# Decoding 64-bit weight words on ScalarE and VectorE: six engine steps rewritten as three

## The chip, the core and the metric

The kernel runs on one core of a Trainium2 chip. The metric is the time of one execution on the device in microseconds (us). A run's time is given as a median of several runs; the profile is one execution of its own, recorded by the hardware profiler.

## The reference

Pooled attention feeds two feed-forward stages. The attention inputs are float32, the five weight matrices are float64.

```python
q_pool = q.reshape(B, H, S // 2, 2, D).mean(axis=3)          # B, H, S, D = 4, 8, 1152, 64
attn = softmax(scale * q_pool @ k.T)                         # 576 queries, 1152 keys per head
x = (attn @ v)  ->  rows of 512, 2304 of them
h = x @ w_in;  x1 = max(0.01 * h, h) @ w_out                 # 512 -> 2048 -> 512
h = max(x1 @ w1, x1 @ w2, x1 @ w3);  out = h @ moe2_w_out    # 512 -> 768 -> 512
```

## The kernel before

Attention works through 16 pairs of heads, four pairs to each of the four batches. For a tile of 128 queries TensorE (PE) makes the scores `s`, VectorE (DVE) takes the row maximum `mx` (line 335), ScalarE (ACT) the exponential `p` (line 336). PE transposes `p` into `pst` and `psf`; ACT copies the first (line 378) and DVE the second (line 385) into `pt`, which PE multiplies with the values (`pv`). Preparing the next pair's keys and queries (`psk`, `psq`, `kt`, `q`) needs PE, ACT (lines 221, 256) and DVE (lines 224, 260). From the fifth pair on there is one score buffer, so the next scores wait for the exponential of the last.

The two feed-forward stages of a batch (`experts`) are interleaved with the attention of the next batch: a generator hands out their matmuls (`m`, `o`) at a fixed ratio to the attention's. The weights are cut into 56 chunks of 128 x 512 numbers. Every activation and every weight is kept as two float32r halves, a rounded one and the rest, and a product is three matmuls.

During batch 0 each chunk is decoded once. `decoded` (line 576) loads it as pairs of 32-bit words into `wraw` (three buffers; line 581, on the SP queue, 512 KB) and turns the pairs into float32 in `wmant` (two buffers). `split_chunk` (line 609) makes the two halves `wsplit` out of it, by a cast on ACT (line 617) and a subtraction on GpSimd (POOL, line 618), and stores them to a scratch buffer in device memory (line 626). Batches 1 to 3 load the halves back. `chunk` keeps the decode 3.75 chunks ahead of its use.

The six steps of `decoded` before, for the words `high` and `low` of a float64:

- line 591, DVE: the 20 fraction bits of `high`, with a one ahead of them, as an integer `m`
- line 594, DVE: `low * 2**-32 + m`, the fraction as a float32, written over `low`
- line 597, DVE: the 11 exponent bits of `high`, into `m`
- line 600, ACT: the exponent shifted to its place in a float32 and re-biased (bias tile `ebias`)
- line 601, DVE: the sign of `high` joined to it, written over `high`
- line 604, POOL: fraction times power of two, into `m`

So `wraw` comes free when line 604 has ended, and `wmant` is held from line 591 to the end of line 618.

Each engine runs its queue in order. The order in the queues is made when the program is built: a scheduler plays the program through with durations of its own and places each instruction where it expects its inputs; the code's order breaks ties, and maxima and exponentials are moved ahead by `tc.high_priority`. A queue so laid out doesn't reorder on the chip: an instruction whose input is late holds all that stand behind it.

Of the kernel before, what the change touches and what calls it, by code (L numbers as in the profile page):

```python
# [7 lines left out]
F32 = mybir.dt.float32  # L8
F32R = mybir.dt.float32r
I32 = mybir.dt.int32  # L10
U32 = mybir.dt.uint32
I64 = mybir.dt.int64
ACTF = mybir.ActivationFunctionType
ALU = mybir.AluOpType
# [8 lines left out]
def kernel(  # L23
# [21 lines left out]
    nc = tc.nc  # L45
# [19 lines left out]
    scale = 0.5 / float(D) ** 0.5  # L65
    NOSYNC = mybir.DependencyInfo(mybir.DependencyClass.NoSync, mybir.DependencyReason.DATA)

    const = ctx.enter_context(tc.tile_pool(name="const", bufs=1))
# [23 lines left out]
    s_mid = ps_5.tile([128, 512], F32, name="s1")  # L92

    ident = const.tile([128, 128], F32, name="ident")
    ebias = const.tile([128, 1], F32, name="ebias")
    rb = [const.tile([128, w], F32, name=f"rb{w}") for w in (X0, T - X0)]
    qt = {}
    for j in range(2):
# [49 lines left out]
    def gap(j):  # L148
        return X0 - 64 * j
# [426 lines left out]
    def decoded(src):  # L576

        raw = wr_p.tile([128, 512, 2], I32, tag="wr", bufs=3, name="wraw")  # L580
        load = nc.sync.dma_start(out=raw.rearrange("p (a f) w -> p a (f w)", a=src.shape[1]), in_=src)
        if len(early) < 2:
            early.append(tc.add_manual_dep(
                load.ins, marks[GATE],
                mybir.DependencyInfo(mybir.DependencyClass.Sync, mybir.DependencyReason.DATA),
                reason="weights behind the first pair",
            ))
        low, high = raw[:, :, 0], raw[:, :, 1]
        m = wr_p.tile([128, 512], I32, tag="wm", name="wmant")
        mf = m.bitcast(F32)  # L590
        nc.vector.tensor_scalar(  # L591
            out=m, in0=high, scalar1=0xFFFFF, scalar2=0x100000, op0=ALU.bitwise_and, op1=ALU.bitwise_or
        )
        nc.vector.scalar_tensor_tensor(  # L594
            out=low.bitcast(F32), in0=low.bitcast(U32), scalar=2.0 ** -32, in1=m, op0=ALU.mult, op1=ALU.add
        )
        nc.vector.tensor_scalar(  # L597
            out=m, in0=high, scalar1=20, scalar2=0x7FF, op0=ALU.logical_shift_right, op1=ALU.bitwise_and
        )
        nc.scalar.activation(out=m, in_=m, func=ACTF.Relu, scale=float(1 << 23), bias=ebias)  # L600
        nc.vector.scalar_tensor_tensor(  # L601
            out=high, in0=high, scalar=-0x80000000, in1=m, op0=ALU.bitwise_and, op1=ALU.bitwise_or
        )
        nc.gpsimd.tensor_tensor(out=mf, in0=low.bitcast(F32), in1=high.bitcast(F32), op=ALU.mult)  # L604
        return mf

    stores = []

    def split_chunk(c):
        src = chunks[c]  # L610
        if wide:
            r = decoded(src)
        else:
            r = wr_p.tile([128, 512], F32, tag="wm", name="wmant")
            nc.sync.dma_start(out=r.rearrange("p (a f) -> p a f", a=src.shape[1]), in_=src)
        t = w_p.tile([128, 2, 512], F32R, tag="w", name="wsplit")
        nc.scalar.copy(out=t[:, 0], in_=r)  # L617
        nc.gpsimd.tensor_tensor(out=t[:, 1], in0=r, in1=t[:, 0], op=ALU.subtract)  # L618
        stores.append((c, t))
        wt[c] = t  # L620
        if len(stores) > 1:
            store_chunk()
# [173 lines left out]
    if True:  # L796
        nc.gpsimd.memset(ident, 0.0)
        nc.gpsimd.affine_select(
            out=ident, in_=ident, pattern=[[-1, 128]], compare_op=ALU.not_equal, fill=1.0, base=0, channel_multiplier=1
        )  # L800
        nc.gpsimd.memset(ebias, -float((1023 - 127 + 20) << 23))
        nc.gpsimd.memset(rb[0][:, 256:X0], 1.0)
        for j in range(2):
            for part in range(2):
                nc.gpsimd.memset(qt[j, part][:, gap(j):gap(j) + 64].bitcast(F32), 0.0)
        moe = None
        roomy = True
        batch = 0
        spent = [0.0, 0.0]

        def advance():
            nonlocal roomy, moe
            d = next(moe, None)
            if d is None:
                moe = None
            elif d == "room":
                roomy = True
            else:
                spent[1] += d

        for c in attention():
            if c == "room":
                while not roomy:
                    advance()
                continue
            if c == "batch":
                while moe is not None:
                    advance()
                moe = experts(batch)
                roomy = False  # L830
                batch += 1
                spent[:] = [0.0, 0.0]
                continue
            done, want = c
            spent[0] += done
            goal = spent[0] * RATIO
            if want is not None:
                goal = min(goal + AHEAD, spent[1] + want)
            while moe is not None and spent[1] < goal:
                advance()  # L840
        while moe is not None:
            advance()
# [30 lines left out]
```

## Time and profile before

| | us |
|---|---|
| median of 3 runs | 1373.49 (1372.48 to 1377.55) |
| span of the profiled execution | 1378.4 |
| PE busy, share of the span | 1274.7 (92%) |
| DVE busy | 729.2 (53%) |
| ACT busy | 638.0 (46%) |
| POOL busy | 357.9 (26%) |

The chunks are decoded between 54 and 539 us, 54 of the 56 after 180 us. The slices of the span in which DVE is busiest (up to 9 tenths) lie in that part; in the second half of the span DVE falls to 4 or 5 tenths and later to 1 or 2. The PE row is lowest in the first third. A share of the whole span is therefore an average over parts with different limits, and the stretch from 180 to 540 us is the one to read. The profiled execution is 4.9 us longer than the median of the timed runs.

### The profile page before, as it was taken

Reading aid. Unit: us, or ns where it says so; the run is one execution under the profiler, and the core shown is the slowest. Engines: PE = TensorE matmul, PEld = TensorE weight load, DVE = VectorE, ACT = ScalarE, POOL = GpSimd, SP = SyncE. Lnnn points to the kernel's source line nnn. Section 1 sums busy time; section 2 is a strip of 40 time slices with the busy share of each in tenths; the row PEclk is TensorE's granted clock in tenths of the full one; section 3 lists DMA queues with packets and bytes.
Section 4 is the critical chain, followed back from the end, with each engine's and each line's share of the span. In section 5 each row is a group of like instructions: output and inputs, shape, how many; then the busy total and the mean of one; then the engine's idle time right before and its main releaser. Section 6 shows DMA issues by size and latency. Waiting matters only on the chain.

```text
span 1378.4 us, 19366 instructions
## 1 busy us (share of the span) xinstructions
PE 1274.7 (92%) x7376; PEld 1024.7 (74%) x7376; DVE 729.2 (53%) x1218; ACT 638.0 (46%) x1253; POOL 357.9 (26%) x322
## 2 busy tenths in 40 slices
PE   5888878789889899999999989999999999999998
PEld 4556646577667678777778868777777788888888
DVE  5756466788897796454645453545555401222110
ACT  5667665556556555353545444444454432112111
POOL 1111034565574554111122110121120102224110
PEclk9999989899899999999999999999999999999999
DMA  5423053756656565353535353443433345333343
GB/s 155 121 73 74 0 148 106 209 199 188 204 190 191 198 205 185 120 155 125 162 124 157 118 149 119 143 142 124 151 121 117 109 138 171 122 123 125 108 134 108
DMA packets 86904, 193.31 MB, mean 140 GB/s; under 512 B 11292, under 2 KB 41756, under 8 KB 86812
## 3 DMA queue, kind: packets, MB, share of 16 engines
q1 hardware_dynamic: 86812, 192.08, 44.6%
q8 instruction: 58, 0.95, 0.3%
q14 instruction: 34, 0.28, 0.1%
HBM read 146.80 MB, written 35.13 MB: 132 GB/s over the span
## 4 chain that ended last, share of the span: by engine, by line
PE 72%; DVE 13%; issue 5%; ACT 5%; POOL 3%; DMA 1%; POOLq 0%; ACTq 0%; DVEq 0%; SPq 0%
PE m L109 38%; PE pv L109 11%; PE s L109 10%; PE pst L109 6%; PE o L109 6%; DVE mx L335 2%; DVE wraw L594 2%; DMA qraw<-in_q_dram 1%; DVE wmant L591 1%; POOL wsplit L618 1%; DVE mx L325 1%; DVE wmant L597 1%; DVE q L260 1%; DVE pt L385 1%; POOL wmant L604 1%
## 5 line engine op out<-in xcount | busy, mean ns | idle before, releaser
L109 PE MATMUL m<-x,w 128*128 128x512 f32 x1224 | 309.6, 398 | 0.0
L109 PEld LDWEIGHTS m<-x,w 128*128 128x128 f32 x1224 | 223.3, 189 | 54.5 <-issue 13.1
L378 ACT COPY pt<-pst 128x512 f32<-128x512 f32 x288 | 167.3, 586 | 187.2 <-PE pst L109 186.2
L109 PE MATMUL s<-kt,q 128*128 128x384 f32 x840 | 190.8, 360 | 27.1 <-ACT p L336 15.0
L335 DVE TENSOR_REDUCE mx<-s 128x1 f32<-128x1152 f32 x108 | 146.3, 1354 | 114.9 <-PE s L109 114.6
L109 PE MATMUL pst<-ident,p 128*128 128x128 f32 x1080 | 170.8, 279 | 14.5 <-DVE pt L385 7.4
L109 PEld LDWEIGHTS s<-kt,q 128*128 128x128 f32 x840 | 149.6, 196 | 38.5 <-ACT p L336 17.0
L109 PEld LDWEIGHTS pst<-ident,p 128*128 128x128 f32 x1080 | 132.7, 143 | 52.6 <-issue 11.9
L739 POOL TENSOR_TENSOR g<-t,g 128x512 fp32r<-128x512 f32 x64 | 84.1, 1315 | 336.5 <-DVE g L738 336.5
L336 ACT ACTIVATE p<-s,mx 128x1152 f32<-128x1152 f32 x108 | 132.3, 1225 | 82.6 <-DVE mx L335 81.8
L109 PE MATMUL pv<-pt,v 128*64 128x320 f32 (+1 forms) x1008 | 154.0, 445 | 12.7 <-DVE pt L385 12.4
L109 PE MATMUL m<-g,w 128*128 128x512 f32 x576 | 149.8, 399 | 0.0
L109 PEld LDWEIGHTS m<-g,w 128*128 128x128 f32 x576 | 103.7, 188 | 24.5 <-issue 6.2
L109 PEld LDWEIGHTS pv<-pt,v 128*64 128x64 f32 x1008 | 69.3, 146 | 70.5 <-issue 22.8
L109 PE MATMUL m<-x,wsplit 128*128 128x512 f32 x408 | 107.4, 403 | 1.2 <-ACT t L765 0.7
L737 ACT ACTIVATE t<-m 128x512 f32<-128x512 f32 x80 | 44.4, 555 | 123.7 <-PE m L109 123.5
L109 PEld LDWEIGHTS m<-x,wsplit 128*128 128x128 f32 x408 | 74.0, 189 | 21.3 <-issue 4.4
L738 DVE CAST g<-t 128x512 fp32r<-128x512 f32 x64 | 32.8, 512 | 102.7 <-ACT t L737 102.2
L618 POOL TENSOR_TENSOR wsplit<-wmant,wsplit 128x512 fp32r<-128x512 f32 x56 | 77.0, 1380 | 34.3 <-ACT wsplit L617 32.2
L604 POOL TENSOR_TENSOR wmant<-wraw 128x512 f32<-128x512 f32 x56 | 61.6, 1100 | 93.3 <-DVE wraw L601 82.1
L677 POOL TENSOR_TENSOR y<-t,y 128x512 fp32r<-128x512 f32 x24 | 32.1, 1339 | 202.1 <-ACT y L676 202.0
L767 DVE TENSOR_TENSOR t<-m,t 128x512 f32<-128x512 f32 (+1 forms) x60 | 38.2, 636 | 84.2 <-PE m L109 73.3
(110 smaller groups left out, 1657.0 us busy)
## 6 DMA issues: line engine op xcount, KB each, us to landing
w<-w SPq DMA_DIRECT2D x168, 512.0 KB
w<-wsplit SPq DMA_DIRECT2D x56, 512.0 KB
wraw<-in_moe_w_out_dram SPq DMA_DIRECT2D x22, 512.0 KB
wraw<-in_moe_w_dram SPq DMA_DIRECT2D x18, 512.0 KB
qraw<-in_q_dram SPq DMA_DIRECT2D x15, 576.0 KB
kraw<-in_k_dram SPq DMA_DIRECT2D x15, 576.0 KB
q<-q SPq DMA_DIRECT2D x52, 160.0 KB
wraw<-in_moe_w_in_dram SPq DMA_DIRECT2D x16, 512.0 KB
```

Source lines behind the costliest of these rows:

```text
L109: mm = f(*args, **kwargs)
L335: nc.vector.tensor_reduce(out=mx[:, 0:1], in_=ps[:, :, 0:SN], axis=AX.XY, op=ALU.max, negate=True)
L336: nc.scalar.activation(out=p[2], in_=ps[:, :, 0:SN], func=ACTF.Exp, bias=mx[:, 0:1], accum_out=rs[:, i:i + 1])
L378: nc.scalar.copy(out=dst, in_=ps.rearrange("p (j c) -> p j c", j=2))
L594: nc.vector.scalar_tensor_tensor(out=low.bitcast(F32), in0=low.bitcast(U32), scalar=2.0 ** -32, in1=m, op0=ALU.mult, op1=ALU.add)
L604: nc.gpsimd.tensor_tensor(out=mf, in0=low.bitcast(F32), in1=high.bitcast(F32), op=ALU.mult)
L618: nc.gpsimd.tensor_tensor(out=t[:, 1], in0=r, in1=t[:, 0], op=ALU.subtract)
L677: nc.gpsimd.tensor_tensor(out=t[:, 1], in0=src, in1=t[:, 0], op=ALU.subtract)
L737: nc.scalar.activation(out=t, in_=ps[:, 0:k.n], func=ACTF.Prelu, alpha=0.01)
L738: nc.vector.tensor_copy(out=gt[:, 0], in_=t)
L739: nc.gpsimd.tensor_tensor(out=gt[:, 1], in0=t, in1=gt[:, 0], op=ALU.subtract)
L767: nc.vector.tensor_tensor(out=t, in0=ps[:, 0:k.n], in1=t, op=ALU.max)
```

## The change

The decode becomes three steps. ACT reads `high` as a float32 and applies a parametric ReLU in place: positive numbers are multiplied by 2^-112, negative ones by 2^-80, which re-biases the exponent field and turns the sign into an exponent bit that the shift below moves to the sign's place. DVE reduces `low` in place to its three top bits, as an integer of 0 to 7. DVE then shifts `high` left by three, joins the three bits, and writes `m`, whose bits are the float32. The tile `ebias` goes, and with it its memset at the start; the line numbers of the changed kernel are one lower ahead of `decoded` and seven lower behind it.

```diff
-        mf = m.bitcast(F32)
-        nc.vector.tensor_scalar(
-            out=m, in0=high, scalar1=0xFFFFF, scalar2=0x100000, op0=ALU.bitwise_and, op1=ALU.bitwise_or
-        )
-        nc.vector.scalar_tensor_tensor(
-            out=low.bitcast(F32), in0=low.bitcast(U32), scalar=2.0 ** -32, in1=m, op0=ALU.mult, op1=ALU.add
-        )
-        nc.vector.tensor_scalar(
-            out=m, in0=high, scalar1=20, scalar2=0x7FF, op0=ALU.logical_shift_right, op1=ALU.bitwise_and
-        )
-        nc.scalar.activation(out=m, in_=m, func=ACTF.Relu, scale=float(1 << 23), bias=ebias)
-        nc.vector.scalar_tensor_tensor(
-            out=high, in0=high, scalar=-0x80000000, in1=m, op0=ALU.bitwise_and, op1=ALU.bitwise_or
-        )
-        nc.gpsimd.tensor_tensor(out=mf, in0=low.bitcast(F32), in1=high.bitcast(F32), op=ALU.mult)
-        return mf
+        nc.scalar.activation(
+            out=high.bitcast(F32), in_=high.bitcast(F32), func=ACTF.Prelu, scale=2.0 ** -112, alpha=2.0 ** 32
+        )
+        nc.vector.tensor_scalar(
+            out=low, in0=low.bitcast(U32), scalar1=2.0 ** -29, scalar2=7.0, op0=ALU.mult, op1=ALU.min
+        )
+        nc.vector.scalar_tensor_tensor(
+            out=m, in0=high, scalar=3, in1=low, op0=ALU.logical_shift_left, op1=ALU.bitwise_or
+        )
+        return m.bitcast(F32)
```

In the changed kernel the ReLU is line 589, the reduction of `low` line 592 and the joining line 595. `wraw` now comes free at the end of line 595, on DVE, and `wmant` is held only from line 595 on. Lines 589 and 592 wait for the chunk's load, line 595 for a free `wmant`, that is, for line 618 of two chunks earlier.

The scheduler lays the queues out anew, with small shifts on PE and larger ones on the others. Two places show it; the numbers at the names are buffers, other ones in each program.

The DVE queue ahead of a maximum and a `psf` copy of the fifth pair, some 70 instructions after the third chunk's first step. Before:

```order
L224 TENSOR_TENSOR kt1_2190<-psq_2293,kt1_2190 64x128
L601 SCALAR_TENSOR_TENSOR wraw_2396<-wraw_2396,wmant_2398 128x512
L591 TENSOR_SCALAR wmant_2435<-wraw_2433 128x512
L594 SCALAR_TENSOR_TENSOR wraw_2433<-wraw_2433,wmant_2435 128x512
L597 TENSOR_SCALAR wmant_2435<-wraw_2433 128x512
L335 TENSOR_REDUCE mx_2376<-s_1743 128x1
L385 COPY pt_2233<-psf_2341 128x6x64
```

And after, where `wraw_2537` is loaded into the buffer of `wraw_2439`:

```order
L223 TENSOR_TENSOR kt1_2164<-psq_2261,kt1_2164 64x128
L595 SCALAR_TENSOR_TENSOR wmant_2441<-wraw_2439 128x512
L334 TENSOR_REDUCE mx_2341<-s_1741 128x1
L384 COPY pt_2204<-psf_2306 128x6x64
L592 TENSOR_SCALAR wraw_2537<-wraw_2537 128x512
L223 TENSOR_TENSOR kt1_2164<-psk_2311,kt1_2164 64x512 x2
L422 TENSOR_TENSOR xf_2353<-pv_2058,rb320_121 128x320
L592 TENSOR_SCALAR wraw_2588<-wraw_2588 128x512
```

Four decode steps stood between the keys and the maximum, and one does now; new are the two steps on line 592, which stand a few instructions behind the step that frees a buffer for a load.

The ACT queue ahead of the exponential of the same maximum. Before:

```order
L617 CAST wsplit_2405<-wmant_2398 128x512
L600 ACTIVATE wmant_2435<-wmant_2435,ebias_121 128x512
L378 COPY pt_2233<-pst_2335 128x2x256
L221 CAST kt1_2190<-psk_2346 64x512 x2
L336 ACTIVATE p_2377,sums_2378<-s_1743,mx_2376 128x1152
```

And after:

```order
L610 CAST wsplit_2367<-wmant_2363 128x512
L377 COPY pt_2204<-pst_2255 128x2x256
L377 COPY pt_2204<-pst_2300 128x2x256
L220 CAST kt1_2164<-psk_2311 64x512 x2
L589 ACTIVATE wraw_2537<-wraw_2537 128x512
L335 ACTIVATE p_2342,sums_2343<-s_1741,mx_2341 128x1152
```

The decode's ACT step has moved from behind a DVE step of its own chunk to a place right ahead of the exponential, where it waits for a load.

## Rows read from the trace of the kernel before

**Rows 1.** Windows: stretch, length, busy PE, PEld, DVE, ACT, POOL, then PEclk, DMA.

```profile
180.00:540.00 360.00, 315.72 (x1702) 242.21 (x1702) 292.41 (x412) 211.20 (x392) 196.56 (x164) 0.93 0.60 189
600.00:960.00 360.00, 349.76 (x2033) 280.86 (x2032) 182.51 (x318) 164.51 (x305) 55.87 (x43) 1.00 0.45 138
```

**Rows 2.** Waits of PE, 180-540 us: total us, times, longest.

```profile
PE s L109 <- ACT p L336: 10.8, 5, 3.5
...
PE psk L109 <- DVE pt L385: 0.3, 1, 0.3
```

**Rows 3.** Timeline around one wait: start, us, engine, line, operation, idle before.

```profile
262.50 1.41 DVE L594 SCALAR_TENSOR_TENSOR wraw<-wraw,wmant 128x512 f32<-128x512 uint32 x1
...
263.38 2.87 POOL L206 TENSOR_TENSOR qraw<-qraw 72x512 f32<-72x512 f32 x2
...
263.94 2.59 DVE L597 TENSOR_SCALAR wmant<-wraw 128x512 int32<-128x512 int32 x1
...
266.45 1.34 DVE L335 TENSOR_REDUCE mx<-s 128x1 f32<-128x1152 f32 x1
...
268.32 1.12 PE L109 MATMUL pst<-ident,p 128*128 128x128 f32 x4 [4.74 <-DVE pt L385]
```

**Rows 4.** PE timeline, a wait with no decode step ahead of it.

```profile
210.24 0.97 PE L109 MATMUL s<-kt,q 128*128 128x384 f32 x4 [2.86 <-ACT p L336]
```

**Rows 5.** Groups of `pv` matmuls, 180-540 us and 600-1100 us.

```profile
L109 PE MATMUL pv<-pt,v 128*64 128x320 f32 (+1 forms) x252 | 42.9, 484 | 5.9 <-DVE pt L385 5.9
...
L109 PE MATMUL pv<-pt,v 128*64 128x320 f32 (+1 forms) x492 | 69.4, 417 | 5.2 <-DVE pt L385 5.2
```

**Rows 6.** Groups of decode, 180-540 us: busy us, mean ns, idle before.

```profile
L594 DVE SCALAR_TENSOR_TENSOR wraw<-wraw,wmant 128x512 f32<-128x512 uint32 x54 | 53.7, 994 | 1.3
...
L601 DVE SCALAR_TENSOR_TENSOR wraw<-wraw,wmant 128x512 int32<-128x512 int32 x54 | 50.0, 927 | 12.4 <-ACT wmant L600 12.3
L591 DVE TENSOR_SCALAR wmant<-wraw 128x512 int32<-128x512 int32 x54 | 39.5, 732 | 16.1 <-POOL wsplit L618 16.0
L597 DVE TENSOR_SCALAR wmant<-wraw 128x512 int32<-128x512 int32 x54 | 34.4, 637 | 0.9
...
L600 ACT ACTIVATE wmant<-wmant,ebias 128x512 int32<-128x512 int32 x54 | 39.1, 724 | 58.4 <-DVE wmant L597 53.1 <-DVE sums L351 2.8 <-DVE sums L350 2.3
L617 ACT CAST wsplit<-wmant 128x512 fp32r<-128x512 f32 x56 | 34.4, 621 | 17.5 <-POOL wmant L604 15.9 <-PE m L109 1.6
...
L604 POOL TENSOR_TENSOR wmant<-wraw 128x512 f32<-128x512 f32 x54 | 59.4, 1100 | 76.5 <-DVE wraw L601 65.3 <-DVE sums L350 7.2 <-DMA wraw<-in_moe_w_out_dram 2.0
```

**Rows 7.** Instructions on tile `wraw`, whole span: minimum, median, maximum ns.

```profile
L591 DVE TENSOR_SCALAR wmant<-wraw x56: 408/420/1526, 54.2 to 531.1; 128x512 int32<-128x512 int32 x56
L594 DVE SCALAR_TENSOR_TENSOR wraw<-wraw,wmant x56: 679/694/1775, 55.1 to 531.5; 128x512 f32<-128x512 uint32 x56
```

**Rows 8.** Groups by form, whole span: ACT writing the pooled queries.

```profile
L256 ACT ACTIVATE q<-psq 64x160 fp32r<-64x160 f32 x58 | 28.9, 498 | 6.8 <-PE psq L109 6.5
...
L256 ACT ACTIVATE q<-psq 64x128 fp32r<-64x128 f32 x58 | 25.3, 436 | 17.6 <-PE psq L109 16.0 <-DVE kt L224 1.1
```

**Rows 9.** Timeline of loads: issue on SP, then the first instruction on the data.

```profile
492.23 2.03 SPq L581 DMA_DIRECT2D wraw<-in_moe_w_out_dram  x2
...
497.63 0.41 DVE L591 TENSOR_SCALAR wmant<-wraw 128x512 int32<-128x512 int32 x1
...
433.65 0.33 SPq L172 DMA_DIRECT2D qraw<-in_q_dram  x1
...
443.19 2.52 POOL L206 TENSOR_TENSOR qraw<-qraw 72x512 f32<-72x512 f32 x2 [3.35 <-DMA qraw<-in_q_dram]
```

**Rows 10.** Waits of DVE and ACT on decode steps, 180-540 us.

```profile
DVE wmant L591 <- POOL wsplit L618: 16.0, 10, 3.3
DVE wraw L601 <- ACT wmant L600: 12.3, 19, 1.3
...
ACT wmant L600 <- DVE wmant L597: 53.1, 34, 5.4
```

More of the change, by code (lines that the diff above doesn't have):

```diff
@@ L94 @@
     ident = const.tile([128, 128], F32, name="ident")
-    ebias = const.tile([128, 1], F32, name="ebias")
     rb = [const.tile([128, w], F32, name=f"rb{w}") for w in (X0, T - X0)]
@@ L800 @@
         )
-        nc.gpsimd.memset(ebias, -float((1023 - 127 + 20) << 23))
         nc.gpsimd.memset(rb[0][:, 256:X0], 1.0)
```

## The prediction

> **What bounds the kernel now.** First I read the page's slices to see where the decode runs, then the busy times of the stretch from 180 to 540 us, which holds 54 of the 56 chunks, beside an equally long one from 600 to 960 us that has the same kind of attention and matmuls but no decode. PE is busy 315.7 of 360 us in the first and 349.8 in the second: 44.3 us idle against 10.2. [...] DVE is busy 292.4 us (81%) against 182.5 (51%). So PE sets the end everywhere, but in the decode stretch it is held by others, and what can be won lies there.
>
> Next the waits of PE in that stretch: 15 lines, which add up to the same 44.3 us, all on ACT and DVE (first and last line: [rows 2]). None names the decode: PE waits for exponentials, copies into `pt`, keys. The question is what stood ahead of those in the queues, so I read the timeline ahead of each wait of 0.25 us or more. The longest shows the pattern: a decode step of 1.41 us and one of 2.59 us, held while POOL adds up queries, stand ahead of a maximum, the maximum ahead of a `psf` copy, and PE waits 4.74 us for that copy [rows 3]. Of the 44.3 us, waits of 30.6 us in all have decode steps ahead in the queue of the releaser; the other 13.7 us don't, as the 2.86 us for an exponential whose maximum began as soon as the scores were there [rows 4].
>
> The lower clock costs time too. A `pv` matmul occupies 42.9/252 = 170 ns in the decode stretch and 69.4/492 = 141 ns in the later one, 7.3 us over 252 of them [rows 5]. All of it is bounded by (1.00 - 0.93) x 360 = 25 us [rows 1].
>
> **What the change removes and adds.** Per chunk DVE loses 994 + 927 + 732 + 637 = 3290 ns, or 177.6 us over 54 chunks; POOL loses 1100 ns (59.4 us); ACT loses 724 ns (39.1 us) [rows 6].
>
> It gains two DVE steps. Line 592 has one tensor input, as line 591, whose median is 420 ns and mean 732; line 595 has two, as line 594, median 694 and mean 994 [rows 6, 7]. The excess of the means over the medians comes where POOL works at the same time, as in rows 3. POOL will be busy 196.6 - 59.4 = 137 us instead of 196.6 [rows 1, 6], so I take means nearer the median: 600 and 850 ns, 1450 ns together. The quiet bound is 1114 ns. The upper one is 2 x 994 = 1988 ns, if writing every second word keeps line 592 from the speed of line 591. DVE thus saves 1.84 us a chunk, 99 us in the stretch, with bounds of 70 and 118.
>
> ACT gains the parametric ReLU, SBUF to SBUF with no bias tile. The nearest row is the cast of line 617, 621 ns; line 600 with its bias tile has 724 [rows 6]. A row that speaks against it is line 256, which writes with a step of 32 bytes: from 128 to 160 elements it grows by 62 ns, 1.94 ns each [rows 8], against about 1.2 per element in all for line 617. At that rate 512 elements need some 1180 ns. The ReLU steps by 8 bytes, and DVE's line 594, which also steps by 8 bytes in and out, needs only 694 ns for 512, 1.36 each [rows 7], so I take 620 ns: 33.5 us for 54, which is 6 us less than now. With 1180 ns it is 25 us more, on an engine that is idle 149 us of the stretch [rows 1].
>
> [...]
>
> DMA bytes stay. A chunk's buffer comes free at the end of line 595 and no longer of line 604; on SP the next load still alternates with the stores, which wait for line 618 as before, and the two casts and subtractions of `split_chunk` stay on ACT and POOL. The memset that goes lies in the first us, beside the first loads: nothing. The first five chunks, before 180 us, put three more ACT steps (1.9 us at most) beside attention whose exponentials PE waits for; I count them at nothing, since nothing there is due before 180 us, with 2 us as a bound.
>
> **The new wait.** Lines 589 and 592 now head their queues until a chunk's load has landed. Before, line 591 could not start before a `wmant` was free, long after the load. Now line 592 of a chunk stands only a few DVE instructions (0 to 11, mostly 2 to 6) behind the line 595 that frees its buffer. How long a load takes is bounded from below by nothing, from above by 5.4 us from issue to first use, and a query load of 576 KB beside it took 9.5 us with POOL waiting 3.35 us [rows 9]. Four DVE instructions at some 0.65 us are 2.6 us of work; waits for PE among them lengthen that to perhaps 4.5. So line 592 waits 0 to 3 us, and I take 1 us a chunk. Queued behind it are maxima, `psf` copies and keys, behind line 589 exponentials and `pst` copies, and behind those PE.
>
> [...]
>
> **The sum.** Count as occupied by decode on DVE its busy time and its waits on other decode steps: 177.6 + 16.0 + 12.3 = 206 us now [rows 6, 10]. After: 54 x (1.45 + 1.0) = 132 us, 64%. ACT likewise: 39.1 + 34.4 + 53.1 + 15.9 = 142 us now [rows 6, 10], after 33.5 + 34.4 + 54 = 122. If the 30.6 us of PE waits shrank in proportion to DVE's share, 11 us would go; without the new wait (78/206) 19. A wait of PE appears only where a delay exceeds its slack, so I take the middle, 14 us. The clock follows: 25 x 14/44.3 = 8 us. The new steps before 180 us cost 1 us. Together 14 + 8 - 1 = 21 us. What is late next is the rest that no decode caused, 13.7 us, and the exponentials.
>
> The profiled execution would go from 1378.4 to about 1357. It lies 4.9 us above the median of the timed runs, 1373.5; I carry the difference over: 1352.5 us.
>
> **The rivals.**
>
> *The decode stretch becomes like the later one.* DVE would be busy 292 - 99 = 193 us, about the 182.5 of 600 to 960 us, where PE idles 10.2 us. Then 34 us of idle and up to 25 us of clock could go; with part of both, 33 to 59, I put it at 40: 1333 us. For it speaks the likeness of the loads on DVE; against it, ACT's 205 us and POOL's 137 against 164.5 and 55.9, and loads at 0.60 of the DMA.
>
> *Nothing to speak of.* The waits move to others of equal length: PE's own order puts scores right behind scores [rows 4], line 595 waits in the DVE queue for POOL as line 591 did (16.0 us [rows 10]), and the load waits eat the rest. 1366 to 1378, say 1371.
>
> *Slower, by the load.* If line 592 and line 589 are each held longer than the work between, DVE is blocked by it. It is occupied for 292.4 + 28.3 = 320.7 us now; after, 193 + 54w, where w is the wait a chunk. The two are equal at w = 2.4 us; beyond that this costs. At w = 3.5, possible if a chunk's load takes as long as the query load of rows 9, DVE is occupied 382 us of 360, so the stretch is stretched by 22 us less what PE gains elsewhere, some 7: 1389 us. Against it: most loads were used within 5.4 to 10 us with no wait recorded.
>
> **Chances.** Forecast (gain of 8 to 33 us) 0.51, larger gain 0.17, nothing to speak of 0.19, slower 0.13. A measurement of this kernel tells apart about 0.5%, 6.9 us. So faster 0.68, same 0.19, slower 0.13. The range leaves out the largest gains and the slow rival's core: 1332 to 1377 us.
>
> **What would show it.** Right: lines 592 and 595 at 0.5 to 0.7 and 0.75 to 0.95 us, line 589 near 0.62; DVE busy some 193 us in the decode stretch; PE idle there about 30 us and clock near 0.96; waits of DVE or ACT on `wraw` loads of some 50 us each. Wrong: PE idle near 44 us although DVE is relieved (the second rival), waits on loads above 130 us (the third), or a gain that lies behind 560 us, where the queues hardly differ.

## The result and the profile after

The changed kernel takes **1356.97 us** (median of 4 runs, 1353.38 to 1358.24) against 1374.40 us of the kernel before: 17.4 us less. The ratio of the two on record is **0.9859, 95% interval 0.9838 to 0.9881**, 1.4% or 19 us; it is not the quotient of the two medians, which is 0.9873 and lies inside the interval, so the gain is 17 to 19 us. The forecast was 1352.5 us, 4.5 us too low, and the time lies in its range. On another chip the same kernel gave 0.9870 (below, under "Which engine's wait it was"). One execution there (1439 us, granted clock 0.837, the profiled one) and one with two DVE steps put back (1802 us, 0.649) ran at a much lower clock than the others, and the ratios leave them out.

The time came from where the prediction looked. The page's busy line and the windows of the changed kernel (stretch, length, busy PE, PEld, DVE, ACT, POOL, then PEclk and DMA, as in [rows 1]):

```profile
PE 1259.0 (93%) x7376; PEld 1015.6 (75%) x7376; DVE 627.9 (46%) x1106; ACT 633.5 (47%) x1253; POOL 292.1 (22%) x265
...
180.00:540.00 360.00, 323.40 (x1842) 253.50 (x1844) 201.14 (x316) 215.02 (x407) 132.74 (x110) 0.96 0.62 198
...
600.00:960.00 360.00, 349.65 (x2035) 280.32 (x2034) 185.99 (x327) 164.06 (x308) 53.29 (x41) 1.00 0.45 139
```

The later stretch is as before. In the decode stretch DVE lost 91 us and POOL 64, PE idles 36.6 us instead of 44.3. But the two windows of 360 us no longer hold the same work: after has 1842 matmuls in it, before 1702 [rows 1]. So I end each window where the last matmul on decoded weights ends. First before, then after:

```profile
180.00:554.14 374.14, 329.86 (x1812) 254.58 (x1813) 298.35 (x423) 217.93 (x405) 196.56 (x164) 0.93 0.59 186
```

```profile
180.00:531.93 351.93, 318.01 (x1812) 248.86 (x1813) 198.45 (x312) 211.68 (x401) 132.74 (x110) 0.97 0.62 198
```

Both now hold 1812 matmuls, with 836 ahead of 180 us in either kernel, and after is **22.2 us** shorter; the two profiled spans differ by 23.7 us (1378.4 and 1354.7), 6 us more than the medians. So nearly the whole gain lies in the decode stretch. In these two executions it has two halves: PE idles 44.3 us before and 33.9 after, 10.4 less, and the same matmuls keep PE busy 11.9 us less, at a granted clock of 0.97 instead of 0.93.

The decode steps, which answer to [rows 6, 7] (busy us, mean ns of one, idle before and what ended it):

```profile
L611 POOL TENSOR_TENSOR wsplit<-wmant,wsplit 128x512 fp32r<-128x512 f32 x56 | 74.1, 1327 | 92.8 <-ACT wsplit L610 71.0 <-DVE t L760 11.4 <-PE psf L108 7.1
...
L595 DVE SCALAR_TENSOR_TENSOR wmant<-wraw 128x512 int32<-128x512 int32 x54 | 46.7, 865 | 30.0 <-POOL wsplit L611 29.9
L589 ACT ACTIVATE wraw<-wraw 128x512 f32<-128x512 f32 x51 | 35.0, 686 | 58.3 <-DMA wraw<-in_moe_w_out_dram 24.6 <-DMA wraw<-in_moe_w_dram 17.5 <-DMA wraw<-in_moe_w_in_dram 14.2
...
L610 ACT CAST wsplit<-wmant 128x512 fp32r<-128x512 f32 x56 | 34.7, 622 | 12.0 <-PE m L108 10.1 <-DMA w<-wsplit 0.9 <-DMA qraw<-in_q_dram 0.5
L592 DVE TENSOR_SCALAR wraw<-wraw 128x512 int32<-128x512 uint32 x51 | 26.3, 516 | 58.7 <-DMA wraw<-in_moe_w_out_dram 29.0 <-DMA wraw<-in_moe_w_in_dram 17.0 <-DMA wraw<-in_moe_w_dram 12.6
```

DVE works 73.0 us on the decode instead of 177.6. The new waits are there: DVE idles 58.6 us and ACT 56.3 us until a chunk's load lands. The timeline shows one (start, us, engine, line, operation; in brackets the idle time before it):

```profile
263.43 1.35 DVE L334 TENSOR_REDUCE mx<-s 128x1 f32<-128x1152 f32 x1
...
264.47 1.17 ACT L220 CAST kt<-psk 64x512 fp32r<-64x512 f32 x2
264.70 0.55 DVE L384 COPY pt<-psf 128x384 f32<-128x384 f32 x1
...
268.00 0.68 ACT L589 ACTIVATE wraw<-wraw 128x512 f32<-128x512 f32 x1 [2.36 <-DMA wraw<-in_moe_w_out_dram]
268.02 0.43 DVE L592 TENSOR_SCALAR wraw<-wraw 128x512 int32<-128x512 uint32 x1 [2.77 <-DMA wraw<-in_moe_w_out_dram]
...
268.48 1.39 DVE L223 TENSOR_TENSOR kt<-psk,kt 64x512 fp32r<-64x512 f32 x2
268.71 1.23 ACT L335 ACTIVATE p<-s,mx 128x1152 f32<-128x1152 f32 x1
```

From 265.6 us on, as far as the profile shows, ACT could have run the exponential of line 335 (its maximum had ended at 264.78), and DVE the addition of line 223 (its input `kt` copy had ended at 265.64). Both stood behind a step whose data came at 268.0: for 2.4 us ready work stood blocked on either engine, and started after that step.

The page's chain that ended last shows the exchange. Before, and then after:

```profile
PE 72%; DVE 13%; issue 5%; ACT 5%; POOL 3%; DMA 1%; POOLq 0%; ACTq 0%; DVEq 0%; SPq 0%
```

```profile
PE 75%; DMA 9%; DVE 7%; ACT 4%; issue 3%; POOL 2%; DVEq 0%; SPq 0%; ACTq 0%; POOLq 0%
```

DVE's share fell from 13% to 7%, and DMA's rose from 1% to 9%.

### The profile page after: what moved, and what is told of

Same layout as the page of the kernel before. It is cut to its first block, busy times and chain, and to the rows that moved or that the text cites. A ratio compares the mean times of both kernels' runs of the same rounds, so it can differ in the third digit from the quotient of the medians.

```text
span 1354.7 us, 19162 instructions
## 1 busy us (share of the span) xinstructions
PE 1259.0 (93%) x7376; PEld 1015.6 (75%) x7376; DVE 627.9 (46%) x1106; ACT 633.5 (47%) x1253; POOL 292.1 (22%) x265
## 4 chain that ended last, share of the span: by engine, by line
PE 75%; DMA 9%; DVE 7%; ACT 4%; issue 3%; POOL 2%; DVEq 0%; SPq 0%; ACTq 0%; POOLq 0%
PE m L108 41%; PE pv L108 10%; PE s L108 10%; PE pst L108 6%; PE o L108 6%; DMA wraw<-in_moe_w_out_dram 3%; DMA wraw<-in_moe_w_in_dram 2%; DMA wraw<-in_moe_w_dram 2%; DMA qraw<-in_q_dram 2%; DVE mx L334 1%; DVE wmant L595 1%; DVE mx L324 1%; ACT pt L377 1%; DVE q L259 1%; POOL wsplit L611 1%
## 5 line engine op out<-in xcount | busy, mean ns | idle before, releaser
L108 PE MATMUL pv<-pt,v 128*64 128x320 f32 (+1 forms) x1008 | 149.9, 435 | 14.0 <-DVE pt L384 13.4
L730 ACT ACTIVATE t<-m 128x512 f32<-128x512 f32 x80 | 44.3, 555 | 128.2 <-PE m L108 128.2
L611 POOL TENSOR_TENSOR wsplit<-wmant,wsplit 128x512 fp32r<-128x512 f32 x56 | 74.1, 1327 | 92.8 <-ACT wsplit L610 71.0
L731 DVE CAST g<-t 128x512 fp32r<-128x512 f32 x64 | 28.7, 448 | 111.2 <-ACT t L730 110.7
L354 DVE TENSOR_SCALAR p<-p,sums 128x1152 f32<-128x1152 f32 x76 | 66.2, 870 | 2.7
```

Of the source, the lines that this page charges most:

```text
L108: mm = f(*args, **kwargs)
L354: nc.vector.tensor_scalar(out=x, in0=x, scalar1=rs[:, i:i + 1], scalar2=None, op0=ALU.mult)
L730: nc.scalar.activation(out=t, in_=ps[:, 0:k.n], func=ACTF.Prelu, alpha=0.01)
L731: nc.vector.tensor_copy(out=gt[:, 0], in_=t)
```

## The experiments

**The theory** was the prediction's: the length of DVE's queue sets what PE waits for; POOL's step counts for nothing; the load wait takes part of the gain back. **Rivals**: the gain comes from POOL's step that went, or the load wait is harmless, or it is so dear that a little more of it makes the change a loss. All ratios are to the kernel before on the same chip. The changes are given as diffs against the changed kernel, cut at `...`; the lists that the demands use are shown once. The scheduler lays out the queues of each program anew, so a part of any difference can be order.

### Two DVE steps put back

```diff
+        nc.vector.tensor_scalar(
+            out=low, in0=low, scalar1=7, scalar2=0, op0=ALU.bitwise_and, op1=ALU.bitwise_or
+        )
+        nc.vector.scalar_tensor_tensor(
+            out=low, in0=low, scalar=7, in1=low, op0=ALU.bitwise_and, op1=ALU.bitwise_or
+        )
         nc.vector.scalar_tensor_tensor(
             out=m, in0=high, scalar=3, in1=low, ...
```

> The changed kernel with two of the removed DVE steps put back in each chunk: two steps on the low word that leave its three bits as they are, one of the form of the old line 591 and one of the form of the old line 594. Nothing else differs. Theory (the gain is DVE's queue made shorter): DVE busy from 180 to 540 us rises from 201 to about 275 us, PE idle there from 36.6 to 42 to 48 us, and 10 to 18 us of the 17 us gained are lost: 1367 to 1375 us against 1357 of the changed kernel. Rival (the gain is POOL's multiplication, or the earlier release of the buffers, or a luckier order): the two steps cost no more than 3 us, 1357 to 1360 us.

Measured: 1376.39 us, ratio 0.9986 [0.9967, 1.0006]. The whole gain is gone; the time lies 1.4 us above the range of the theory, on a chip on which the kernel before took 1379.38. The stretch and the two steps' groups in it:

```profile
180.00:540.00 360.00, 316.97 (x1759) 245.78 (x1756) 263.48 (x410) 210.68 (x400) 137.48 (x110) 0.95 0.59 193
...
L598 DVE SCALAR_TENSOR_TENSOR wraw<-wraw 128x512 int32<-128x512 int32 x51 | 44.7, 877 | 1.0
...
L595 DVE TENSOR_SCALAR wraw<-wraw 128x512 int32<-128x512 int32 x51 | 23.7, 464 | 1.1
```

They leave every value as it is and use no other engine, yet 68.4 us of DVE work cost 17.5 us of time (0.0127 of 1376; the intervals leave 13 to 22). PE idles 43.0 us instead of 36.6, inside the 42 to 48 expected; DVE is busy 263 us, less than the 275 expected. With them DVE's four decode steps are busy 145.6 us, against 73.0 in the changed kernel. The gain is a gain of DVE's queue.

### POOL's step put back

```diff
-    func=ACTF.Prelu, scale=2.0 ** -112, alpha=2.0 ** 32
+    func=ACTF.Prelu, scale=2.0 ** -113, alpha=2.0 ** 32
...
+        nc.gpsimd.tensor_tensor(out=m.bitcast(F32), in0=m.bitcast(F32), in1=m.bitcast(F32), op=ALU.add)
         return m.bitcast(F32)
```

> The changed kernel with a POOL step put back at the end of the decode: the ReLU multiplies by half as much (2^-113) and POOL adds the number to itself, in place, so the chain of a chunk has its sixth engine step again and POOL its 1.1 us a chunk. DVE has its two steps. Theory (DVE's queue): 0 to 5 us are lost, from DVE steps held beside POOL: 1357 to 1362 us, PE idle from 180 to 540 us at 36 to 40 us. Rival (POOL's step was what counted, by the held DVE steps and by the length of the chain): 10 to 17 us are lost, 1367 to 1374 us.

The weights of this kernel come out as 1/128 of themselves; the number and size of its steps are as said. Measured: 1358.87 us, ratio 0.9869 [0.9835, 0.9902]. Nothing is lost, although POOL is busy 58 us more and DVE's steps become slower beside it:

```profile
L598 POOL TENSOR_TENSOR wmant<-wmant 128x512 f32<-128x512 f32 x54 | 58.4, 1083 | 47.6 <-DVE wmant L595 33.5 <-DVE sums L349 8.3 <-DMA w<-wsplit 2.6
...
L595 DVE SCALAR_TENSOR_TENSOR wmant<-wraw 128x512 int32<-128x512 int32 x54 | 50.5, 939 | 23.7 <-POOL wsplit L612 23.5
...
L592 DVE TENSOR_SCALAR wraw<-wraw 128x512 int32<-128x512 uint32 x51 | 32.7, 640 | 53.5 <-DMA wraw<-in_moe_w_out_dram 26.8 <-DMA wraw<-in_moe_w_dram 17.9 <-DMA wraw<-in_moe_w_in_dram 8.6
```

Line 595 grew from 865 to 939 ns and line 592 from 516 to 640, 10 us in all on DVE. By the price of the experiment above that is 2.5 us, less than the interval can show. The 10 to 17 us of the rival are excluded: POOL's own step was not on the path. The earlier release of `wraw` was not put back by itself. Before the change no wait of DVE or ACT in the stretch names a load, and POOL waited 2.0 us for one [rows 6], so an earlier load had next to nothing to win.

### No decode at all

The three steps are left out; `decoded` returns the high words as they are.

> The changed kernel without the three decode steps: the high words go to the cast and the subtraction as they are, so the numbers are not the weights; loads, halves, stores and all matmuls stay. It bounds what any decode can still win. Theory: DVE falls to about 130 us and the head-of-queue waits on loads fall on ACT's cast alone; PE idle from 180 to 540 us goes from 36.6 to 15 to 25 us, the granted clock to 0.98; 1338 to 1347 us. Rival (what is left is PE's own order and the exponentials): PE idle stays above 30 us, 1351 to 1357 us.

Measured: 1328.47 us, ratio 0.9646 [0.9617, 0.9674]: 49 us is all that the decode steps cost before, and the change got 19 of it. I had expected 1338 to 1347. PE still idles 18 us in the stretch:

```profile
180.00:540.00 360.00, 341.54 (x1986) 271.36 (x1988) 148.38 (x236) 201.03 (x381) 136.27 (x115) 0.98 0.67 210
```

### Both load waits taken away by order

The steps that read a load are placed later in their queues, by two demands on order alone: the low word's step behind the join (line 595's operation) of the chunk before, the ReLU behind the cast two chunks earlier. Every step stays. The low word's step now stands 6 to 22 DVE instructions behind the join that frees its buffer, where it stood 0 to 11 behind.

```diff
-        nc.scalar.activation(
+        relu = nc.scalar.activation(
...
-        nc.vector.tensor_scalar(
+        bits = nc.vector.tensor_scalar(
...
+        if len(joins) > 4:
+            tc.add_manual_dep(bits.ins, joins[-1].name, NOSYNC, reason="behind the load")
+            tc.add_manual_dep(relu.ins, casts[-2].name, NOSYNC, reason="behind the load")
-        nc.vector.scalar_tensor_tensor(
+        join = nc.vector.scalar_tensor_tensor(
...
+        joins.append(join.ins)
...
-        nc.scalar.copy(out=t[:, 0], in_=r)
+        casts.append(nc.scalar.copy(out=t[:, 0], in_=r).ins)
```

> The changed kernel with another place in the queues for the two steps that wait for a load: the reduction of the low word behind the joining step of the chunk before, the ReLU behind the cast of the chunk two before. These are demands on the order alone, no waits. Theory (the new waits on loads cost what the prediction gave them): the waits of DVE and ACT on loads, 58.6 and 56.3 us from 180 to 540 us, fall below 15 us each, PE idle falls by 3 to 8 us, and so does the time: 1347 to 1354 us. Rival (those waits stand in time that the engines have to spare): the waits fall and the time doesn't, 1355 to 1359 us. Second rival: the chain of a chunk gets too long and PE waits for weights, over 1359 us.

Measured: 1343.63 us, ratio 0.9762 [0.9728, 0.9797]. It is below the 1347 to 1354 us of the theory. Once more, on another chip:

> The version with both order demands once more, with more rounds, on the chip of the two runs above. It came out at 1343.6 us. If that holds: 1340 to 1347 us, ratio 0.973 to 0.980, load waits near zero on both engines. If it was that chip: 1348 to 1356 us.

Measured: 1346.13 us, ratio 0.9784 [0.9769, 0.9798]. So it holds, and it is faster than both kernels: the load waits had cost 10 to 13 us (0.0075 to 0.0097 of 1375; the intervals leave 7 to 19). Its decode groups and its chain, from the second run:

```profile
L600 DVE SCALAR_TENSOR_TENSOR wmant<-wraw 128x512 int32<-128x512 int32 x54 | 47.5, 880 | 41.5 <-POOL wsplit L617 41.1
...
L591 ACT ACTIVATE wraw<-wraw 128x512 f32<-128x512 f32 x51 | 34.6, 678 | 0.0
...
L594 DVE TENSOR_SCALAR wraw<-wraw 128x512 int32<-128x512 uint32 x51 | 29.7, 583 | 0.0
```

```profile
PE 81%; DVE 8%; ACT 5%; issue 2%; DMA 2%; POOL 1%; SPq 0%; ACTq 0%; DVEq 0%; POOLq 0%
```

Neither engine waits for a load any more, and DMA falls from 9% of the chain to 2%. The join now waits 41 us for POOL, whose subtraction frees its output buffer, 11 us more than in the changed kernel.

### Which engine's wait it was

Three kernels on one chip: the changed kernel itself, and each of the two demands alone.

> The changed kernel itself, on the chip on which the next three run, so that they can be set beside it. Both theories: 1353 to 1360 us, ratio 0.984 to 0.989; waits of DVE and of ACT on the weight loads near 58 us each between 180 and 540 us, PE idle there 35 to 38 us.

Measured: ratio 0.9870 [0.9834, 0.9906], as on the first chip. The waits that were expected are not read from this run.

The demand on DVE alone:

```diff
+            tc.add_manual_dep(bits.ins, joins[-1].name, NOSYNC, reason="behind the load")
```

> Of the two order demands that took the load waits away, only the one on DVE: the low word's step behind the join of the chunk before; the ReLU on ACT still heads its queue until the load has landed. If DVE's wait is what counted (DVE being the engine whose steps stand ahead of PE's maxima and copies): most of the 13 us, 1345 to 1350 us, DVE's load waits under 5 us, ACT's near 60 us as before. If ACT's wait is what counted (PE's largest wait of the changed kernel, 12.6 us, names exponentials of ACT): 1354 to 1358 us. If each engine's wait costs its share: about 1350 to 1353.

Measured: 1358.62 us, ratio 0.9873 [0.9842, 0.9904]. No gain that the intervals show (they leave some 7 us either way), though DVE's load wait is gone:

```profile
L599 DVE SCALAR_TENSOR_TENSOR wmant<-wraw 128x512 int32<-128x512 int32 x54 | 48.4, 896 | 47.8 <-POOL wsplit L616 47.4
L591 ACT ACTIVATE wraw<-wraw 128x512 f32<-128x512 f32 x51 | 34.6, 678 | 55.1 <-DMA wraw<-in_moe_w_out_dram 20.6 <-DMA wraw<-in_moe_w_dram 20.5 <-DMA wraw<-in_moe_w_in_dram 11.7
...
L594 DVE TENSOR_SCALAR wraw<-wraw 128x512 int32<-128x512 uint32 x51 | 30.7, 602 | 0.0
```

The demand on ACT alone:

```diff
+            tc.add_manual_dep(relu.ins, casts[-2].name, NOSYNC, reason="behind the load")
```

> The other demand alone: the ReLU on ACT behind the cast two chunks earlier; the low word's step on DVE still heads its queue until the load has landed. If DVE's wait counted: 1353 to 1357 us, DVE's load waits still 40 to 58 us, ACT's under 10 us. If ACT's wait counted: 1345 to 1350 us. Shared: 1350 to 1353.

Measured: 1350.52 us, ratio 0.9812 [0.9783, 0.9841]: some 8 us, on the border of what was written down for ACT's wait and for shared waits.

```profile
L599 DVE SCALAR_TENSOR_TENSOR wmant<-wraw 128x512 int32<-128x512 int32 x54 | 45.6, 845 | 18.0 <-POOL wsplit L616 14.5 <-ACT pt L377 3.3
L591 ACT ACTIVATE wraw<-wraw 128x512 f32<-128x512 f32 x51 | 34.7, 680 | 0.0
...
L594 DVE TENSOR_SCALAR wraw<-wraw 128x512 int32<-128x512 uint32 x51 | 29.0, 568 | 55.1 <-DMA wraw<-in_moe_w_out_dram 26.0 <-DMA wraw<-in_moe_w_dram 18.2 <-DMA wraw<-in_moe_w_in_dram 10.6
```

I had put DVE first. It was ACT's wait that was dear: its demand gave 8 us more than DVE's on the same chip, and the two intervals do not overlap. DVE's demand shows no gain while ACT still waits, and perhaps 4 us (0.0028 of 1376, from 0.9812 to 0.9784, on different chips, within the intervals) once ACT's wait is gone. It also traded one wait for another: the join's wait for POOL rose from 29.9 to 47.4 us, while ACT's demand let it fall to 17.8 us for POOL and ACT together.

Exponentials stand behind the ReLU on ACT, and PE's largest wait of the changed kernel names them; both demands bring it down from 12.6 to 7.6 us:

```profile
PE s L108 <- ACT p L335: 12.6, 7, 4.0
```

```profile
PE s L108 <- ACT p L335: 7.6, 5, 2.9
```

That line alone proves little: it is 9.7 us with the demand on DVE alone and 8.7 with POOL's step put back, and neither of those kernels gained. That the exponentials are the way by which ACT's wait reaches PE is likely, not shown.

### The low word's step left out, and moved to POOL

The first kernel drops the step of line 592, so that DVE has one step with one tensor input. The second keeps all steps and both demands, but runs the low word's step on POOL.

Left out:

```diff
-        nc.vector.tensor_scalar(out=low, ...)
-        nc.vector.scalar_tensor_tensor(
-            out=m, in0=high, scalar=3, in1=low, op0=ALU.logical_shift_left, op1=ALU.bitwise_or
+        nc.vector.tensor_scalar(
+            out=m, in0=high, scalar1=3, scalar2=0, op0=ALU.logical_shift_left, op1=ALU.bitwise_or
         )
```

> The step on the low word is left out, and with it the three lowest bits of every weight: per chunk the ReLU on ACT and one shift with one tensor input on DVE remain. If the length of DVE's queue is what counts (two steps put back cost 17 us, so one step is worth 8 to 9 us): 1345 to 1350 us, DVE busy between 180 and 540 us some 30 us less. If, now that DVE is short, the load wait on ACT is what holds PE (the order demand on DVE alone gained nothing): 1353 to 1358 us, although DVE is relieved, ACT's load waits still near 58 us.

Measured: 1350.36 us, ratio 0.9811 [0.9797, 0.9825]. A gain, 0.4 us above the times that the queue's length asked for, in spite of 59.4 us of load waits left on ACT. DVE's decode falls from 73.0 to 32.8 us of work and loses its load wait besides, and that brings 7 us; at a quarter of a us for each us of work alone it would be 10. The 3 us between them lie within the intervals, so whether ACT's wait held part of it is not shown.

On POOL, as a diff against the kernel with both demands:

```diff
-        bits = nc.vector.tensor_scalar(
+        bits = nc.gpsimd.tensor_scalar(
...
-            tc.add_manual_dep(bits.ins, joins[-1].name, NOSYNC, reason="behind the load")
+            tc.add_manual_dep(bits.ins, subs[-2].name, NOSYNC, reason="behind the load")
```

(`subs` lists the subtractions on POOL.)

> The version with both order demands, and the low word's step moved from DVE to POOL, placed there behind the subtraction two chunks earlier. POOL gets some 54 x 1.1 = 59 us of work between 180 and 540 us, DVE loses 54 x 0.58 = 31 us but its other steps slow down beside POOL (with a POOL step put back, the join grew from 865 to 939 ns). If DVE's queue still counts: 1336 to 1342 us. If DVE's joins now wait for a later POOL, or POOL's queries and subtractions come late: DVE waiting for POOL 60 us and more, 1344 to 1360 us.

Measured: 1338.54 us, ratio **0.9725 [0.9707, 0.9744]**, the fastest kernel of this study, 7.6 us below the version with both demands on the same chip.

```profile
L595 POOL TENSOR_SCALAR wraw<-wraw 128x512 int32<-128x512 uint32 x51 | 105.2, 2062 | 4.3
...
L601 DVE SCALAR_TENSOR_TENSOR wmant<-wraw 128x512 int32<-128x512 int32 x54 | 44.1, 818 | 41.6 <-POOL wraw L595 41.0
```

The step takes 2062 ns on POOL, twice what I expected and 3.5 times the 583 ns on DVE, and still it pays: 33 us less decode work on DVE bring 8 us (the intervals leave 5 to 11), again about a quarter of a us for each. The slower DVE steps that I expected beside a busier POOL did not come: the join takes 818 ns, against 880 with both demands.

### More load wait

Two buffers for raw weights, then one, instead of three: a load is issued later.

```diff
-        raw = wr_p.tile([128, 512, 2], I32, tag="wr", bufs=3, name="wraw")
+        raw = wr_p.tile([128, 512, 2], I32, tag="wr", bufs=2, name="wraw")
```

> Two buffers for raw weights instead of three: a chunk's load is issued when the join two chunks earlier is done, not three. It lengthens the disputed wait and nothing else. If the load wait grows with it and blocks both queues (the rival that ends slower): waits of 130 us and more on the loads of DVE and of ACT between 180 and 540 us, 1375 to 1400 us. If the time between one chunk's steps and the next still covers the load (one chunk each 6.7 us, 4.1 us to landing): waits of 60 to 90 us, 1357 to 1366 us.

Measured: 1363.10 us, ratio 0.9907 [0.9875, 0.9940], whose interval overlaps that of the changed kernel on the same chip. The waits hardly grew (58.1 us on DVE, 58.7 on ACT), and the order in the queues moved along with the buffers: line 592 stands 0 to 9 DVE instructions behind the join that frees its buffer, as against 0 to 11 with three buffers. It did not lengthen what it was to lengthen, so it says nothing on the price. One buffer did:

```diff
+        raw = wr_p.tile([128, 512, 2], I32, tag="wr", bufs=1, name="wraw")
```

> One buffer for raw weights instead of three, so that a load cannot be issued before the chunk just ahead has been joined; two buffers left the load waits as they were. This makes the load wait long on purpose and tries the price that the prediction gave to its slower rival: DVE occupied 201 us by work between 180 and 540 us and 54 times w by loads, w the mean wait a chunk, break-even with the kernel before at w = 2.4 us. If that price holds: waits of DVE on loads above 130 us make it slower than the kernel before, 1385 to 1410 us at w = 3.5 to 4. If such waits lie mostly where DVE and ACT would idle anyhow: 1360 to 1375 us in spite of waits above 130 us. If the waits stay near 60 us, the load is not what fixes them: 1357 to 1368 us.

Measured: 1383.95 us, ratio **1.0041 [1.0024, 1.0057]**: slower than the kernel before.

```profile
180.00:540.00 360.00, 310.57 (x1657) 237.34 (x1654) 192.26 (x303) 205.09 (x390) 131.20 (x108) 0.93 0.58 187
...
L589 ACT ACTIVATE wraw<-wraw 128x512 f32<-128x512 f32 x53 | 36.2, 683 | 80.0 <-DMA wraw<-in_moe_w_out_dram 37.0 <-DMA wraw<-in_moe_w_in_dram 21.5 <-DMA wraw<-in_moe_w_dram 21.4
L592 DVE TENSOR_SCALAR wraw<-wraw 128x512 int32<-128x512 uint32 x53 | 29.0, 548 | 98.7 <-DMA wraw<-in_moe_w_out_dram 36.5 <-DMA wraw<-in_moe_w_dram 32.8 <-DMA wraw<-in_moe_w_in_dram 29.0
```

The steps are the short ones, DVE is busy only 192 us, and PE idles 49 us at a clock of 0.93: all that the short queue gave is taken back by 98 us of load waits on DVE and 80 on ACT. None of the three outcomes that I had written down came: the loss came at 98 us of DVE waits, not above 130, and it is a small one.

### All runs side by side

Between 180 and 540 us, in us; "waits for others" are waits of DVE's decode steps for POOL or ACT. The last matmuls on decoded weights start at the time in the column "ends", in us of the profiled execution; some 2650 matmuls lie ahead of their end in each kernel.

| kernel | DVE decode work | DVE waits for loads | DVE waits for others | ACT waits for loads | ends | ratio |
|---|---|---|---|---|---|---|
| before [rows 6, 10] | 177.6 | 0 | 28.3 | 0 | 554 | 1 |
| changed | 73.0 | 58.6 | 29.9 | 56.3 | 532 | 0.9859 |
| two DVE steps back | 145.6 | 36.6 | 19.6 | 61.1 | 551 | 0.9986 |
| POOL step back | 83.2 | 53.3 | 23.5 | 53.8 | 531 | 0.9869 |
| demand on DVE | 79.1 | 0 | 47.4 | 52.8 | 528 | 0.9873 |
| demand on ACT | 74.6 | 54.8 | 17.8 | 0 | 525 | 0.9812 |
| both demands (second run) | 77.2 | 0 | 41.1 | 0 | 520 | 0.9784 |
| low step left out | 32.8 | 0 | 55.5 | 59.4 | 524 | 0.9811 |
| both, low step on POOL | 44.1 | 0 | 41.0 | 0.9 | 514 | 0.9725 |
| two buffers | 76.5 | 58.1 | 21.5 | 58.7 | 537 | 0.9907 |
| one buffer | 71.4 | 98.3 | 9.1 | 79.9 | 564 | 1.0041 |
| no decode | 0 | 0 | 0 | 2.9 | 504 | 0.9646 |

No single column of work or waits orders the rows. Work on DVE and load waits on ACT together nearly do; the row with one buffer fits least. The ends order them almost as the ratios do, the demand on DVE apart, which ends 4 us ahead of the changed kernel and shows no gain in time: what these kernels differ by lies in the decode stretch.

## Why the prediction was right

**Where the time is.** Right. 22.2 of the 23.7 us between the profiled executions lie in the decode stretch.

**PE waits 14 us, clock 8 us.** The sum agrees with the profiled executions, 10.4 and 11.9, but some 6 us of that agreement is chance: the profiled execution before lies 4.0 us above its median and the one after 2.3 below, and the medians differ by 17.4 us, not by 23.7. The clock's half was larger than the proportion gave it: with 23% of PE's idle time gone, the granted clock went from 0.93 to 0.97, more than half of the way to 1.00. The clock does not follow the idle time in proportion: between 180 and 540 us PE idles 27.2 us with the low word's step left out, at a clock of 0.95, and 36.6 us in the changed kernel, at 0.96.

**DVE's share as the measure of PE's waits.** Right in direction; its size came out by two errors that offset each other. The rule counts DVE's decode work and its waits on loads and other decode steps, 206 us before. For after it took 132 us, 64%, and put the wait of line 595 for a free `wmant` at nothing without a reason. That wait was 29.9 us, so DVE was occupied 73.0 + 58.6 + 29.9 = 161.5 us, 78%. With this the rule gives 30.6 x 0.22 = 6.6 us of PE waits, 3.7 of clock and, less the 1 us lost, 9 us in all, half of what was measured. The second error is its price, (30.6/206) x (1 + 25/44.3) = 0.23 us of time for each us of occupied DVE; 17.4 us for 206 - 161.5 = 44.4 us is 0.39. The 0.24 that the experiments show is another price, of work alone: 17.5 us for the 72.6 us of two steps put back, 8.1 for the 33.1 moved to POOL. With the waits, which fell as the two steps came in, two steps put back cost 17.5 for 201.8 - 161.5 = 40.3 us, 0.43. Nor does DVE's occupied time settle the time alone: it is 126.5 us with the demand on DVE and 147.2 with the demand on ACT, which is 8 us faster.

**The steps.** Line 595 measured 865 ns (850 taken), line 592 516 ns (600 taken; its median 430 is near the 420 of line 591 in spite of writing every second word, so the bound of 1988 ns falls). The ReLU took 686 ns where 620 were taken, 3.4 us over the stretch. The rate of line 256 (1180 ns) is excluded. The cast of as many dense elements took 622 ns, but that is another operation, so what the ReLU's step of two float32 costs by itself was not shown.

**The new wait: 1 us a chunk.** Its length was right: 58.6/54 = 1.09 us on DVE, 1.04 on ACT, "some 50 us each" forecast. Its price was put at the difference between 29 and 21 us, 8 us, by taking 14 us between the proportion's 11 and 19 on the argument that a delay shows only beyond its slack. Taking both waits away gave 10 to 13 us. That leans towards the proportion, but the intervals, 7 to 19 us, do not exclude 8. Those runs also lengthened the join's wait for POOL by 11 us, so that the waits by themselves may be dearer. The sum with 11 instead of 14 would be 11 + 6 - 1 = 16 us and hit the measured time, but by luck, since the wait for POOL is missing there too. The prediction also put the price on DVE, while the wait on ACT was the dearer.

**A load.** The prediction had one load's 5.4 us from issue to first use as its bound from above. The loads on `wraw` of the changed kernel landed after 4.1 us in the median, 6.0 at most:

```profile
DMA to landing us min/median/max: 3.6/4.1/6.0
```

**The rivals.** *Like the later stretch*, 1333 us: no, even with no decode at all it is 1328. *Nothing to speak of*: no, though one of its moves came true: line 595 waits for POOL longer (29.9 us) than line 591 did (16.0 [rows 10]). *Slower, by the load*: not here, but its mechanism is real, and it decides earlier than the prediction said. It put the break-even at w = 2.4 us a chunk, by DVE's time alone. Between the changed kernel (58.6 us, 1.41% faster) and the one with one buffer (98.3 us, 0.41% slower) a straight line crosses zero at 58.6 + 39.7 x 1.41/1.82 = 89 us, or 1.65 us a chunk. That is an estimate: the one buffer also puts a chunk's steps in a row (the join waits 9.1 us for the ReLU). The formula left out that ACT waits for the same loads, and that line 595 waits for POOL.

**What stays open.** Why taking away DVE's wait shows no gain while ACT's is there was not tried further; that both feed the same join is an argument, not a measurement. A third buffer for the join's output, to take away the 41 us for which it waits for POOL, was not tried.

## What to carry to other kernels

When an edit shortens a queue that others stand in, look at what now heads it: the first step on fresh data used to wait for an output buffer (16.0 us in the stretch, none for a load), and its load had landed by then. Rewritten in place it needs none, heads its queue, and blocks all that stands behind it until the load lands (58.6 us of waits on DVE, 56.3 on ACT). Placing these steps some places later, by order alone, brought 10 to 13 us on top of the 17 to 19 of the whole change, and no step had to be faster for it. And price a step by its queue, not by its length: a step that takes 583 ns on the crowded engine was well placed at 2062 ns on one with time to spare.

## What the runs showed of the hardware

- The same operation on 128 x 512 elements, each row with a step of two words, took 583 ns on DVE and 2062 on POOL (1962 at the least), where POOL's float32 additions of as many dense elements took 1083.
- DVE's steps were longer beside POOL. In the kernel before, line 591 (one tensor input) took a mean of 0.42 us in the 22 cases of the stretch in which POOL ran nothing beside it, and 0.96 us in the 31 in which POOL ran for more than half of its time; line 594 took 0.69 and 1.24 us. More POOL work in the stretch did not always go with longer steps: the join took a mean of 880 ns with both demands, at 134 us of POOL work, and 818 ns with the low word's step on POOL, at 252 us.
- The same 512 KB load took a median of 3.7 us to landing with one buffer, 4.1 with three, and 7.2 with no decode, at DMA shares of 0.58, 0.62 and 0.67 in the stretch.
